# The last pair's finer t1 sums of x in a freed part of xT, and new unit orders for the second expert

## The chip, the core and the metric

The kernel runs on one core of a Trainium2 chip. The core has five engines that work at the same time: TensorE (PE, matrix products, with a row PEld for its weight loads), VectorE (DVE), ScalarE (ACT), GpSimd (POOL) and SyncE (SP, here a queue that issues DMAs). The on-chip memory SBUF has 128 partitions; products land in PSUM, eight banks of 128 x 512 fp32. The metric is device time in microseconds (us), lower is better.

## The reference

Two parts follow each other. The first is an attention with exponential features, whose output is the 4608 x 512 matrix x. The second is a layer of eight experts that all see every token; the weights P come from alternate normalisation of rows and columns.

```python
def phi(x):
    proj = np.einsum('bhsd,df->bhsf', x, w_phi)
    proj = proj - np.max(np.abs(proj), axis=-1, keepdims=True)
    return np.concatenate([np.exp(proj), np.exp(-proj)], axis=-1)
...
N, D = x.shape                  # 4608, 512; E = 8 experts, F = 1024
logits = x @ w_gate
logits = logits - logits.max()
P = np.exp(logits)
for _ in range(8):
    P /= P.sum(1, keepdims=True) + 1e-09
    P /= P.sum(0, keepdims=True) + 1e-09
    P *= N / E
out = np.zeros((N, D), dtype=np.float32)
for e in range(E):
    h = np.maximum(x @ w1[e], 0.0)
    ye = h @ w2[e]
    out += P[:, e:e + 1] * ye
```

## The kernel before

**Tiles.** x is kept transposed in bf16, xT, as four rows of 128 features by 4608 tokens. The tokens make nine groups of 512; groups 0 to 7 form four pairs, (0,1) to (6,7), and group 8 stands alone.

**Seven products for eight.** From the second expert on (e = 1, with `up7` and `down7`), both matrix products of an expert use Strassen's scheme in Winograd's form: of four blocks of each operand, some sums are made first, and seven products do the work of eight. `sums_x` makes the sums of x, once for all experts: t2, t3 and t4 go into tiles of the ring X, and t1 replaces a block of xT in place. From the third expert on (`up49`), three of these seven products ("11", "21" and t1 of x) are split once more in the same way, and for that `fine_x` makes four finer sums of each of the three blocks, into one more tile of the ring X. All of these are stored to DRAM (xd for t2 to t4, xi for the finer ones, xi6t being those of t1 of the pair (6,7)), and later experts load them back into xT, which is free then (`load_fine`). `sums_up` and `sums_down` make the sums of an expert's weights, `fine_up` the finer ones.

**Rings.** X has four tiles. In the second expert three of them hold t2, t3 and t4 of the pair at work until the products have read them. The fourth takes, one after another, the three sets of finer sums: each set has to be stored before the next can be written there. From the third expert on the ring's memory holds other things (K).

**Units.** An expert is a row of units: for each pair two (one for each half of the hidden features), and one for group 8. A unit's products of the first matrix are named x1, w1, x2, x3, w2, y1 and x4 with 0 or 1 behind, those of the second matrix, of a group that is one or two units back, X1, Y1, Z1, X2, X3, Z2, X4. A product goes into a PSUM bank, and ACT or DVE empties it: the products x4 add to a bank whose x3 result DVE has first to read with the addition at L1530. The results of the second matrix are added to acc, on DVE (L1860), or by ACT (L1872) and POOL (L1875).

**What sets the order.** `UNITS` holds, for each unit, a string in which steps are written; `turns` says which string each unit of each expert takes (entries 0 to 8 are the second expert's). From the strings a planner (`Plan`) makes the order of instructions on every engine: it goes through modelled time, and where several instructions could start, the one written first goes first. It knows the data that instructions read and write by keys: reads wait for the last write of a key, writes for its reads too. Each engine, and the SP and POOL queues, then work strictly in the planned order. The weights of the third expert (e = 2) are loaded by POOL (L517), behind its addition of step Y1 of group 4, and DVE makes their sums (T<-w, w<-w) in the last two units of the second expert.

**Places in xT.** `space` names a stretch of a row of xT that is used again once the products with that part of x are done. `FINE_W` are three such places for weight sums, `PLAIN_X` five and `FINE_X` four for loaded sums of x; `PLAIN_X.places[4]` is the first 1024 columns of the fourth row, which held features of the pair (0,1).

Of the kernel before, what the change touches and what calls it, by code (L numbers as in the profile page):

```python
# [12 lines left out]
ALU = mybir.AluOpType  # L13
# [113 lines left out]
class Links:  # L127
# [13 lines left out]
    def step(self, t, work):  # L141
        on = [n for n in range(2) if self.line[n] and self.line[n][0][0] <= t + 1e-9]
        later = [x[0][0] for n, x in enumerate(self.line) if x and n not in on]
        if not on:
            return (min(later), None, None) if later else None
        share = [1.0, 1.0]
        if len(on) == 2:
            a, b = (x[0][2] for x in self.line)
            all_ = (0.61 if a.turn else 0.84) / (a.unit + b.unit)
            share = [all_ * a.unit, all_ * b.unit]  # L150
        dt, n = min((work[n] / share[n], n) for n in on)
        if later and later[0] - t < dt:
            dt, n = max(later[0] - t, 0.0), None
        for i in on:
            work[i] -= dt * share[i]
        return t + dt, n, work
# [193 lines left out]
def kernel(  # L350
# [77 lines left out]
    def dma(queue, nbytes, rate, fn, r=(), w=()):  # L428

        speed, unit = LINK.get(rate, (rate, 40))  # L430
        if nbytes == 2 << 20:
            speed, unit = 400, 150
        o = plan.op(queue, 0.8 if queue == "POOL" else 0.6, 0.0, fn, r, w, (), nbytes / speed)
        o.turn, o.unit = rate == 148, unit
# [71 lines left out]
    def new(tag):  # L506
        return R[tag].new()
# [582 lines left out]
    def stage_g(b):  # L1090
# [11 lines left out]
    order = (  # L1102
        "lraeaepqbwlqaqawwabwmqlltnrbppnwqbppmrmanbqaqmwwacmpnpbccpwbtcnmqnaqbclupunm"
        "taumquglcapalbcpnqqdcenmucugbblnapmrcqdutabnqpmunpbambccddnqplanmqmducpblttb"
        "augnaqlnrbdcampcadmqeutunqcppmdcaqtdqabpbbmlrqtdnpmuaqualbnagnacctbmqulupran"
        "tdpmtdqcmdnpdabdancpcabbqmpumqbcdgnappqunburqcbugmmnqdcdanumupqbnucmcpnmbddp"
        "bqmpncncubncmmgccg"
    )
# [127 lines left out]
    def sub(eng, el, out_, x, y, op, r, w):  # L1236
        f = nc.vector if eng is dve else nc.gpsimd
        kw = {"shared": True} if eng is dve else {}
        eng(el * 0.5 if eng is dve else el * 1.04 + 128,
            lambda: f.tensor_tensor(out=out_(), in0=x(), in1=y(), op=op), r, w, **kw)  # L1240
# [30 lines left out]
    def fine_up(A, n):  # L1271

        f, r = A[n]
        t, key, first = FINE_W[n]

        def a(q, k):
            return lambda: f()[:, k, :].rearrange("p (f q c) -> p q f c", f=2, q=2)[:, q]

        def s(n):
            return lambda: t()[:, n]  # L1280

        def step(n, x, y, op, r, w):
            sub(dve, 256, s(n), x, y, op, r, [(key, n), *w])

        step(0, a(1, 0), a(1, 1), ALU.add, r, first)
        step(2, a(0, 0), a(1, 0), ALU.subtract, r, [])
        step(1, s(0), a(0, 0), ALU.subtract, [*r, (key, 0)], [])
        step(3, a(0, 1), s(1), ALU.subtract, [*r, (key, 1)], [])
        A[n + "*"] = t, [(key, i) for i in range(4)]
# [34 lines left out]
    def xall(gs):  # L1324
        return [k for g in gs for k in xkeys(g)]

    def space(row, at, n, names, dims, dtype=BF16):

        def make():
            t = xT[:, row, at:at + n]  # L1330
            t = t.bitcast(dtype) if dtype != BF16 else t
            return t.rearrange(f"p ({' '.join(names)}) -> p {' '.join(names)}",
                               **dict(zip(names, dims)))

        first = [k for p in range(at // 1024, (at + n - 1) // 1024 + 1) for k in xall(pairs[p])]
        return make, ("space", row, at), first

    class Turns:
# [4 lines left out]
        def next(self):  # L1343
# [9 lines left out]
    PLAIN_X = Turns([space(2 + i // 4, 1024 * (i % 4), 1024, "akc", (2, 2, 256))  # L1353
                     for i in range(5 if len(INNER) > 2 else 6)])
# [5 lines left out]
    Xi = {(g[0], n): dram.tile([128, 7, 256], BF16, name=f"xi{g[0]}{n}")  # L1360
          for g in pairs for n in INNER.values()}
# [3 lines left out]
    def fine_x(gs, n, b, r0):  # L1365

        g = gs[0]
        r = xall(gs) + ["late", *r0]
        dma("SP", 1 << 16, 160, lambda: nc.sync.dma_start(
            out=Xi[g, n][:, 0, :], in_=b()[:, 0, 0, :]), r, [("Xi", g, n, 0)])  # L1370
        dma("SP", 1 << 17, 160, lambda: nc.sync.dma_start(
            out=Xi[g, n][:, 1:3, :], in_=b()[:, :, 1, :]), r, [("Xi", g, n, 1)])
        y = new("X")

        def t(n):
            return lambda: y().rearrange("p a k c -> p (a k) c")[:, n]

        def blk(k, a):
            return lambda: b()[:, a, k, :]

        sub(dve, 256, t(0), blk(0, 1), blk(0, 0), ALU.subtract, r, [(y, 0), "order of X"])
        sub(dve, 256, t(2), blk(1, 1), blk(0, 1), ALU.subtract, r, [(y, 2)])
        sub(dve, 256, t(1), blk(1, 1), t(0), ALU.subtract, [*r, (y, 0)], [(y, 1)])
        sub(dve, 256, t(3), blk(1, 0), t(1), ALU.subtract, [*r, (y, 1)], [(y, 3)])
        dma("SP", 1 << 18, 160, lambda: nc.sync.dma_start(
            out=Xi[g, n][:, 3:7, :], in_=y().rearrange("p a k c -> p (a k) c")),
            [(y, i) for i in range(4)], [("Xi", g, n, 2)])

    def load_fine(gs):

        g, X = gs[0], {}

        def move(name, d, r, turns, part=None):
            t, key, first = turns.next()
            X[name] = t, [key]
            size = (512 if part else 1024) if turns is PLAIN_X else 1792
            dma("SP", size << 8, 160, lambda: nc.sync.dma_start(
                out=t()[:, 0:part] if part else t(), in_=d()), r, [key, *first, "order of X"])

        if len(gs) == 1:  # L1400
            for n in (2, 3, 4):
                move(f"t{n}", lambda n=n: Xd[g, n][:, 0:1], [("Xd", g, n)], PLAIN_X, 1)
            return X
        for n in ("11", "t1", 2, "21", 3, 4, "22"):
            if n == "22" or n in ("11", "21", "t1") and n not in INNER.values():
                move(n, lambda n=n: Xp[g, n], [("Xp", g, n, a) for a in range(2)], PLAIN_X)
            elif isinstance(n, int):
                move(f"t{n}", lambda n=n: Xd[g, n], [("Xd", g, n)], PLAIN_X)
            else:
                move(n, lambda n=n: Xi[g, n], [("Xi", g, n, i) for i in range(3)], FINE_X)  # L1410
        return X
# [379 lines left out]
    def down7(e, g, H, B7):  # L1791
# [173 lines left out]
    def next_down():  # L1965
        if early:
            return early.pop(0)
        e, g, H, B7, w2, ns = wait.pop(0)
        d = down8(e, g, H, w2) if (e, g) == (E - 1, 7) else down7(e, g, H, B7)
        d["slots"] = ns  # L1970
        return d
# [7 lines left out]
    for e in range(1, E):  # L1979
# [13 lines left out]
        for n, gs in enumerate(turn):  # L1993
            if (e, n) == (1, 4):
                plan.inorder = 1
            X = nextX if e == 1 else load_fine(gs)
# [27 lines left out]
    last = next_down()  # L2024
# [34 lines left out]
```

## Time and profile before

| | |
|---|---|
| median of 3 runs | 1010.66 us (1009.91 to 1011.52) |
| profiled execution, its span | 1008.8 us |
| PE busy | 994.0 us (99%) |
| DVE busy | 898.6 us (89%) |
| ACT busy | 812.8 us (81%) |
| POOL busy | 447.6 us (44%) |

The profile is of one execution; it gives the span from the first to the last instruction, which is 1.86 us less than the median of the runs, and no other time of its own. Rows name the engine, the line of the kernel, the operation, and the tiles written and read, as in `X<-xT`. "Idle before" with an engine or DMA behind it says what the engine waited for. The record of a matmul or of a DVE instruction ends after the next one has begun, so groups of equal instructions are read by their starts.

### The profile page before, as it was taken

To read this page: it belongs to the slowest core of one execution; us is meant where nothing else is said; L and a number is where in the kernel's file an instruction comes from. 1 tells how busy PE (TensorE), PEld (TensorE's weight loads), DVE (VectorE), ACT (ScalarE), POOL (GpSimd) and SP (SyncE) were. 2 spreads that over 40 slices of the span, in tenths; PEclk is the share of its full clock that TensorE was granted. 3 is DMA by queue.
4 is the path that set the end of the run, shared out by engine and by line. 5 is a ranking of instruction groups with operands and counts; after the bars stand their busy time and mean duration, and the time that the engine had idled before them with its cause. 6 is when DMAs were issued, how large, how long until landed. Compare 5 with 4: busy or idle time off the path is not lost.

```text
span 1008.8 us, 23309 instructions
## 1 busy us (share of the span) xinstructions
PE 994.0 (99%) x8376; PEld 727.7 (72%) x8376; DVE 898.6 (89%) x1999; ACT 812.8 (81%) x1930; POOL 447.6 (44%) x514
## 2 busy tenths in 40 slices
PE   7899999999999999999999999999999999999998
PEld 5666666644566877777777877787778777787775
DVE  7999998987888998899989898989889988989886
ACT  7999999845979788878878788777887888778874
POOL 5778674400133344434444444444443444344443
PEclk9999999999999999999999999999999999999999
DMA  9999999181136423282327133632246222724653
GB/s 249 183 202 183 157 153 144 38 170 56 53 121 143 147 97 98 84 184 96 109 98 170 44 100 131 130 127 98 97 117 177 97 98 84 147 79 142 208 174 126
DMA packets 129748, 128.86 MB, mean 128 GB/s; under 512 B 55776, under 2 KB 98272, under 8 KB 129632
## 3 DMA queue, kind: packets, MB, share of 16 engines
q1 hardware_dynamic: 97680, 103.33, 36.3%
q0 software_dynamic: 31648, 23.86, 16.9%
q8 instruction: 65, 1.06, 0.5%
q14 instruction: 51, 0.42, 0.2%
q10 hardware_dynamic: 304, 0.20, 0.1%
HBM read 122.50 MB, written 19.53 MB: 141 GB/s over the span
## 4 chain that ended last, share of the span: by engine, by line
PE 92%; DVE 3%; ACT 2%; DMA 2%; issue 1%; POOL 0%; DVEq 0%
PE ps L1466 41%; PE ps L1475 20%; PE ps L622 17%; PE ps L1607 11%; PE ps L905 2%; DMA xi6t<-X 1%; DMA xi<-X 1%; PE ps L752 1%; ACT q L618 0%; DVE m L614 0%; ACT k L618 0%; DVE wx L614 0%; DVE X L1240 0%; DMA acc<-in_k_dram 0%; DVE hs L1676 0%
## 5 line engine op out<-in xcount | busy, mean ns | idle before, releaser
L1875 POOL TENSOR_TENSOR acc<-acc,hx 128x512 f32<-128x512 f32 x186 | 236.1, 1276 | 404.7 <-ACT hx L1872 135.0
L1466 PEld LDWEIGHTS <-hs 128*128 128x128 bf16 x1984 | 194.1, 98 | 46.4 <-issue 0.2
L1872 ACT ACTIVATE hx<-ps,P 128x256 f32<-128x256 f32 x372 | 158.9, 483 | 53.4 <-PE ps L1466 52.0
L1860 DVE SCALAR_TENSOR_TENSOR acc<-ps,P,acc 128x256 f32<-128x256 f32 x372 | 162.2, 478 | 30.2 <-PE ps L1466 28.2
L1475 PE MATMUL ps<-xT,T 128*128 128x512 bf16 x608 | 171.0, 379 | 0.0
L1466 PEld LDWEIGHTS <-hx 128*128 128x128 bf16 x1488 | 145.6, 98 | 24.9
L1466 PE MATMUL ps<-hx,hs 128*128 128x256 bf16 x992 | 144.3, 273 | 0.0
L1676 DVE CUSTOM_DVE_ANT_0 hs<-ps,U 128x512 bf16<-128x512 f32 x192 | 124.7, 684 | 11.3 <-PE ps L1475 6.6
L1607 PE MATMUL ps<-xT 128*128 128x256 bf16 x576 | 125.4, 272 | 0.0
L1475 PEld LDWEIGHTS <-T 128*128 128x128 bf16 x672 | 65.8, 98 | 40.6
L1682 ACT ACTIVATE hs<-ps 128x512 bf16<-128x512 f32 x96 | 55.9, 598 | 41.7 <-PE ps L1475 40.2
L1466 PE MATMUL ps<-wx,hs 128*128 128x256 bf16 x560 | 78.4, 273 | 0.0
L622 PE MATMUL ps<-w,hx 128*128 128x512 bf16 x288 | 73.0, 379 | 0.0
L622 PE MATMUL ps<-xT,w 128*128 128x512 bf16 x288 | 72.9, 379 | 0.0
L1466 PE MATMUL ps<-wx,hx 128*128 128x256 bf16 x496 | 72.3, 273 | 0.0
L1676 DVE CUSTOM_DVE_ANT_0 hs<-ps,X 128x512 bf16<-128x512 f32 x96 | 65.1, 684 | 7.8 <-PE ps L1607 6.9
L1466 PE MATMUL ps<-hx 128*128 128x256 bf16 x496 | 71.2, 273 | 0.0
L1607 PEld LDWEIGHTS <-xT 128*128 128x128 bf16 x576 | 56.3, 98 | 17.5
L1466 PE MATMUL ps<-w,hx 128*128 128x256 bf16 x432 | 62.2, 273 | 0.0
L614 DVE TENSOR_REDUCE m<-ps 128x4 f32<-128x512 f32 x88 | 58.8, 680 | 3.7 <-PE ps L622 1.9
L1672 ACT COPY X<-ps 128x512 f32<-128x512 f32 x96 | 58.6, 610 | 2.5 <-DVE ps L1650 2.5
L1466 PE MATMUL ps<-w,hs 128*128 128x256 bf16 x432 | 60.2, 273 | 0.0
(174 smaller groups left out, 2256.0 us busy)
## 6 DMA issues: line engine op xcount, KB each, us to landing
xT<-xi SPq DMA_DIRECT2D x48, 448.0 KB, 4.6
xT<-xd SPq DMA_DIRECT2D x72, 256.0 KB, 4.0
wx<-in_moe_w_dram POOLq DMA_DIRECT2D x8, 1024.0 KB, 11.2
v_m<-in_v_dram SPq DMA_DIRECT2D x15, 512.0 KB, 5.2
out_dram<-acc SPq DMA_DIRECT2D x14, 512.0 KB, 3.0
w<-in_moe_w_dram POOLq DMA_DIRECT2D x6, 1024.0 KB, 11.0
xT<-xp SPq DMA_DIRECT2D x24, 256.0 KB, 2.8
qk<-in_k_dram POOLq DMA_DIRECT2D x12, 256.0 KB, 5.4
```

The costliest lines, as they stand in the source:

```text
L614: dve(el, lambda: nc.vector.tensor_reduce(out=dst(), in_=src(), axis=AX.X, op=ALU.max, apply_absolute_value=True), r, w)
L622: nc.tensor.matmul(out_, lhsT=lhsT, rhs=rhs, start=start, stop=stop)
L905: pe(65, lambda j=j: nc.tensor.matmul(pn()[:, j * D1:j * D1 + D1], lhsT=s["T"][x]()[:, j % 2, 2 * h + j // 2, :] if j < 4 else r["T"][x]() ...
L1466: pe(256, lambda i=i, k=k, z=z: nc.tensor.matmul(bank()[:, 256 * i:256 * i + 256], lhsT=lhs(k, i), rhs=rhs(k), start=first and z, stop=k = ...
L1475: pe(512, lambda k=k: nc.tensor.matmul(bank().rearrange("p (a b) -> p a b", a=2), lhsT=lhs(k), rhs=rhs(k), start=first and k == 0, stop=k ...
L1607: pe(256, lambda: nc.tensor.matmul(halves_of(bank[q], n)(), lhsT=lhs(), rhs=t()[:, rhs, :], start=start, stop=True, skip_group_check=True) ...
L1672: act(512, lambda: nc.scalar.copy(out=flat(to[q])(), in_=bank[q]()), [bank[q]], [(to[q], 0), (to[q], 1)])
L1676: dve(515, lambda: nc.vector._custom_dve(ADD_SAT, out=out_(q, i, j), in0=bank[q]().rearrange("p (a b) -> p a b", a=2), in1=to[q](), s0=3.0 ...
L1682: act(512, lambda: nc.scalar.activation(out=out_(q, i, j), in_=bank[q]().rearrange("p (a b) -> p a b", a=2), func=ACT.Relu, bias=0.0, scal ...
L1860: dve(320, lambda n=n, ts=ts: nc.vector.scalar_tensor_tensor(out=acc[g][:, ts, 256 * j:256 * j + 256], in0=bank()[:, 256 * n:256 * n + 256 ...
L1872: act(370, lambda n=n: nc.scalar.activation(out=u()[:, n, :], in_=bank()[:, 256 * n:256 * n + 256], func=ACT.Copy, bias=0.0, scale=P[:, 4 ...
L1875: pool(695, lambda: nc.gpsimd.tensor_tensor(out=acc[g][:, 2 * i:2 * i + 2, 256 * j:256 * j + 256], in0=acc[g][:, 2 * i:2 * i + 2, 256 * j: ...
```

## The change

Two things change in the code, and one in the tables. In `fine_x`, the four finer sums of t1 of the pair (6,7) are written to `PLAIN_X.places[4]` instead of a tile of X, and stored from there. In `fine_up`, sum 2 gets the same first wait as sum 0, for the readers of the part of xT that it overwrites. Of `UNITS`, the entries 4 to 8 are written anew (those that follow are only wrapped differently).

```diff
@@ fine_up
         step(0, a(1, 0), a(1, 1), ALU.add, r, first)
-        step(2, a(0, 0), a(1, 0), ALU.subtract, r, [])
+        step(2, a(0, 0), a(1, 0), ALU.subtract, r, first)
         step(1, s(0), a(0, 0), ALU.subtract, [*r, (key, 0)], [])
@@ fine_x
-        y = new("X")
-
-        def t(n):
-            return lambda: y().rearrange("p a k c -> p (a k) c")[:, n]
+        last = g == 6 and n == "t1"
+        if last:
+            y, key, first = PLAIN_X.places[4]
+            keys = [[key, *first]] * 4
+        else:
+            y, first = new("X"), []
+            keys = [[(y, i)] for i in range(4)]
+
+        def t(i):
+            return lambda: y().rearrange("p a k c -> p (a k) c")[:, i]
...
-        sub(dve, 256, t(0), blk(0, 1), blk(0, 0), ALU.subtract, r, [(y, 0), "order of X"])
+        sub(dve, 256, t(0), blk(0, 1), blk(0, 0), ALU.subtract, r, [*keys[0], "order of X"])
...
-            [(y, i) for i in range(4)], [("Xi", g, n, 2)])
+            [k[0] for k in keys], [("Xi", g, n, 2)])
@@ UNITS
-        "x10 x11 w10 x21 x20 Z1 w11 X1 X2 x30 X3 y11 Y1 x31 w21 x41 x40 X4 Z2 w20 y10",
...
+        "x11 w11 w10 x10 X1 y11 x20 Z1 x30 X2 x21 x40 x31 X3 Z2 w20 Y1 w21 X4 x41 y10",
```

The planner makes of this another order of all engines from about 287 us of the trace before to about 354; ahead and behind, the order is as it was. Lines of the change behind `fine_x` are 6 higher (L1530 is L1536, L1860 is L1866). Three places on DVE follow. In the rows, `[waits ...]` names the semaphores an instruction waits on (DMAHW0 to 7 are those of the SP queue, taken in turn; DMASW6 is one of POOL's loads), L1240 is any sum, `w_5163` and `w_5170` are the same tile, w1 of the third expert.

DVE about the end of the last unit of the pair (4,5), where the finer sums of the next pair, (6,7), are made; before, those of t1 are the four into X with the wait on DMAHW0, which is the store of the "21" sums:

```order
L1240 TENSOR_TENSOR hx<-hs,hx 128x512
L1860 SCALAR_TENSOR_TENSOR acc_82<-ps,P,acc_82 128x256 [waits PE_49,Activation_49]
L1860 SCALAR_TENSOR_TENSOR acc_82<-ps,P,acc_82 128x256
L1240 TENSOR_TENSOR X<-xT 128x256 [waits DMAHW0_49,DVE_49]
L1240 TENSOR_TENSOR X<-xT 128x256
L1240 TENSOR_TENSOR X<-xT,X 128x256 [waits DVE_49] x2
L1240 TENSOR_TENSOR hx<-hs 128x512 [waits PE_49] x2
```

The same place now; the four into xT are those of t1:

```order
L1240 TENSOR_TENSOR X<-xT 128x256 [waits DMAHW7_49]
L1240 TENSOR_TENSOR X<-xT 128x256
L1240 TENSOR_TENSOR X<-xT,X 128x256 [waits DVE_49]
L1240 TENSOR_TENSOR xT<-xT 128x256
L1240 TENSOR_TENSOR X<-xT,X 128x256 [waits DVE_49]
L1240 TENSOR_TENSOR xT<-xT 128x256
L1240 TENSOR_TENSOR hx<-hs,hx 128x512
L1240 TENSOR_TENSOR xT<-xT 128x256 [waits DVE_49]
L1866 SCALAR_TENSOR_TENSOR acc_81<-ps,P,acc_81 128x256 [waits PE_49]
```

The t1 sums moved up among the "21" sums (X<-xT and X<-xT,X here), and no DMA is waited for on their account.

DVE at the first sum of group 8, t3 (X<-xT 128x512), before:

```order
L1860 SCALAR_TENSOR_TENSOR acc_82<-ps,P,acc_82 128x256
L1530 ISA hs<-ps,U 128x2x256
L1530 ISA hs<-ps,U 128x2x256 [waits PE_49]
L1240 TENSOR_TENSOR X<-xT 128x512 [waits DMAHW1_49]
L1240 TENSOR_TENSOR hx<-hs,hx 128x512 [waits DVE_49]
L1240 TENSOR_TENSOR xT<-xT 128x2x256 [waits DVE_49]
```

and now:

```order
L1240 TENSOR_TENSOR hx<-hs 128x512
L1240 TENSOR_TENSOR hx<-hs 128x512 [waits PE_49]
L1240 TENSOR_TENSOR X<-xT 128x512 [waits DMAHW0_49]
L1240 TENSOR_TENSOR hs<-hs 128x2x256 [waits DVE_49]
L1536 ISA hs<-ps,U 128x2x256 [waits PE_49,Activation_49]
L1536 ISA hs<-ps,U 128x2x256 [waits PE_49]
```

The sum moved ahead of all four additions of the first unit of the pair (6,7), and waits on DMAHW0 (the store of the "21" sums) where it waited on DMAHW1 (the store of the t1 sums).

DVE at the first sums of the weights of the third expert, in the last unit of the pairs, before:

```order
L1240 TENSOR_TENSOR hs<-hs 128x2x256
L1240 TENSOR_TENSOR hx<-hx,hs 128x512
L1240 TENSOR_TENSOR T<-w_5163 128x1024 [waits DMASW6_49]
L1240 TENSOR_TENSOR X<-xT 128x512 [waits DVE_49,PE_49]
L1240 TENSOR_TENSOR hx<-hs,hx 128x512 [waits DVE_49]
L1240 TENSOR_TENSOR w_5163<-w_5163 128x2x512 [waits DVE_49]
L1240 TENSOR_TENSOR xT<-w_5163 128x256
L1530 ISA hs<-ps,U 128x2x256 [waits PE_49,Activation_49]
L1240 TENSOR_TENSOR X<-xT,X 128x512 [waits DMAHW4_49,DVE_49,PE_49]
```

and now:

```order
L1240 TENSOR_TENSOR hx<-hs,hx 128x512 [waits DVE_49]
L1240 TENSOR_TENSOR X<-xT 128x512 [waits PE_49]
L1240 TENSOR_TENSOR T<-w_5170 128x1024 [waits DMASW6_49]
L1240 TENSOR_TENSOR xT<-w_5170 128x256
L1240 TENSOR_TENSOR w_5170<-w_5170 128x2x512 [waits DVE_49]
L1240 TENSOR_TENSOR xT<-w_5170 128x256
L1240 TENSOR_TENSOR xT<-xT,w_5170 128x256 [waits DVE_49]
L1536 ISA hs<-ps,U 128x2x256 [waits PE_49,Activation_49]
L1240 TENSOR_TENSOR X<-xT,X 128x512 [waits DMAHW4_49,PE_49]
L1536 ISA hs<-ps,U 128x2x256
```

Group 8's second sum (X<-xT 128x512) and one sum of H moved ahead of T<-w, and two more finer weight sums ahead of the additions. On PE, the last product of step Y1 of group 4, behind which POOL issues the weight loads, stands three 256-column matmuls later than before.

More of the change, by code (lines that the diff above doesn't have):

```diff
@@ L1372, in fine_x @@
             out=Xi[g, n][:, 1:3, :], in_=b()[:, :, 1, :]), r, [("Xi", g, n, 1)])
-        y = new("X")
-        def t(n):
-            return lambda: y().rearrange("p a k c -> p (a k) c")[:, n]
+        last = g == 6 and n == "t1"
[7 more added lines that the diff above has]
+            return lambda: y().rearrange("p a k c -> p (a k) c")[:, i]
         def blk(k, a):
             return lambda: b()[:, a, k, :]
-        sub(dve, 256, t(0), blk(0, 1), blk(0, 0), ALU.subtract, r, [(y, 0), "order of X"])
-        sub(dve, 256, t(2), blk(1, 1), blk(0, 1), ALU.subtract, r, [(y, 2)])
-        sub(dve, 256, t(1), blk(1, 1), t(0), ALU.subtract, [*r, (y, 0)], [(y, 1)])
-        sub(dve, 256, t(3), blk(1, 0), t(1), ALU.subtract, [*r, (y, 1)], [(y, 3)])
+        sub(dve, 256, t(0), blk(0, 1), blk(0, 0), ALU.subtract, r, [*keys[0], "order of X"])
+        sub(dve, 256, t(2), blk(1, 1), blk(0, 1), ALU.subtract, r, keys[2])
+        sub(dve, 256, t(1), blk(1, 1), t(0), ALU.subtract, [*r, keys[0][0]], keys[1])
+        sub(dve, 256, t(3), blk(1, 0), t(1), ALU.subtract, [*r, keys[1][0]], keys[3])
         dma("SP", 1 << 18, 160, lambda: nc.sync.dma_start(
             out=Xi[g, n][:, 3:7, :], in_=y().rearrange("p a k c -> p (a k) c")),
-            [(y, i) for i in range(4)], [("Xi", g, n, 2)])
+            [k[0] for k in keys], [("Xi", g, n, 2)])
     def load_fine(gs):
```

20 rows, old and new, of the table UNITS are left out of this document.

## The prediction

> **What bounds the kernel now.** I read the page's busy times, then the busy times by stretch, the waits, the chain and the order of time. The page first:
>
> ```profile
> span 1008.8 us, 23309 instructions
> PE 994.0 (99%) x8376; PEld 727.7 (72%) x8376; DVE 898.6 (89%) x1999; ACT 812.8 (81%) x1930; POOL 447.6 (44%) x514
> ```
>
> TensorE (PE) is busy for 99% of the span, and it has the full clock (the 1.00 behind the engines in the next table). Only its idle time can be won, so the next table asks where that lies. Columns are the stretch, its length, the busy time of PE, its weight loads, DVE, ACT and POOL, the granted clock, the DMA share and GB/s.
>
> ```profile
> 0.00:60.00 60.00, 50.27 (x530) 34.65 (x531) 54.11 (x117) 54.31 (x135) 41.86 (x72) 1.00 1.19 221
> ...
> 220.00:320.00 100.00, 99.64 (x600) 58.03 (x599) 83.60 (x209) 75.12 (x147) 18.43 (x16) 1.00 0.28 89
> 320.00:340.00 20.00, 19.37 (x142) 13.62 (x140) 18.33 (x48) 16.27 (x33) 6.16 (x5) 1.00 1.04 268
> 340.00:990.00 650.00, 649.72 (x5200) 508.49 (x5198) 585.91 (x1259) 520.28 (x1267) 283.21 (x271) 1.00 0.41 116
> ```
>
> The change reorders work from about 287 to 354 us alone; before and behind, the instructions stand as they did. There PE is idle for 0.63 us, all of it between 320 and 340. The 9.73 us at the start and the 3.83 us behind 990 are not touched. The idle 0.63 us has one owner, found in the waits from 290 to 336 us (in total, times, longest):
>
> ```profile
> DVE X L1240 <- DMA xi6t<-X: 1.0, 1, 1.0
> PE ps L1475 <- DVE hs L1530: 0.6, 1, 0.6
> ```
>
> The chain ties the two waits together:
>
> ```profile
> 317.00 7.75 DMA xi6t<-X
> ...
> 324.77 0.42 DVE X L1240
> ...
> 329.13 0.42 DVE X L1240
> 329.55 0.61 DVE hs L1530
> ...
> 330.20 0.59 PE ps L1475 x2
> ```
>
> The store of the last pair's t1 sums (xi6t<-X) takes 7.75 us to land. It holds the fourth tile of the ring of sum tiles, because the other three hold the pair's t2, t3 and t4, which products still read. So group 8's first sum waits for it on VectorE (DVE), everything behind it on DVE is late, and at last PE waits for a DVE addition that empties its bank. What PE loses is more than the 0.6 us of that row, since a matmul's record overlaps the next one:
>
> ```profile
> 321.84 1.03 PE L1475 MATMUL ps<-X,wx 128*128 128x512 bf16 x4
> 322.71 1.89 PE L1475 MATMUL ps<-xT,wx 128*128 128x512 bf16 x8
> 329.20 0.38 PE L1475 MATMUL ps<-xT,T 128*128 128x512 bf16 x1
> 330.20 1.19 PE L1475 MATMUL ps<-X,wx 128*128 128x512 bf16 x4 [0.62 <-DVE hs L1530]
> 331.67 1.04 PE L1466 MATMUL ps<-hx,hs 128*128 128x256 bf16 x8
> ```
>
> From the first row, matmuls of 512 columns follow each other every (1.03 - 0.38) / 3 = 0.217 us; from the last, those of 256 every (1.04 - 0.27) / 7 = 0.11 us. The one behind 329.20 was due at 329.42 and began at 330.20: 0.78 us. The next four took 1.19 instead of 1.03: 0.16 us. The stall costs 0.94 us.
>
> **The change, part by part.** First DVE in order of time (start, length of the group, idle time before it). A record overlaps the next by some 0.08 us: two additions take 1.28 in the last row, so one holds the engine for 0.60, and a sum of 0.42 holds it for 0.34.
>
> ```profile
> 313.08 1.01 DVE L1240 TENSOR_TENSOR hx<-hs,hx 128x512 bf16<-128x512 bf16 x1
> 315.17 0.88 DVE L1860 SCALAR_TENSOR_TENSOR acc<-ps,P,acc 128x256 f32<-128x256 f32 x2 [1.08 <-PE ps L1466]
> 315.96 0.49 DVE L1240 TENSOR_TENSOR X<-xT 128x256 bf16<-128x256 bf16 x2
> 316.36 0.61 DVE L1240 TENSOR_TENSOR X<-xT,X 128x256 bf16<-128x256 bf16 x2
> ...
> 318.14 0.42 DVE L1240 TENSOR_TENSOR hx<-hs 128x512 bf16<-128x512 bf16 x1 [0.83 <-PE ps L1466]
> ...
> 324.77 0.42 DVE L1240 TENSOR_TENSOR X<-xT 128x512 bf16<-128x512 bf16 x1 [1.01 <-DMA xi6t<-X]
> 325.12 0.42 DVE L1240 TENSOR_TENSOR hx<-hs,hx 128x512 bf16<-128x512 bf16 x1
> ...
> 326.46 0.69 DVE L1240 TENSOR_TENSOR T<-w 128x1024 bf16<-128x1024 bf16 x1
> ...
> 329.47 1.28 DVE L1530 CUSTOM_DVE_ANT_0 hs<-ps,U 128x512 bf16<-128x512 f32 x2
> ```
>
> The SP queue and POOL in order of time:
>
> ```profile
> 308.03 4.68 SPq L1385 DMA_DIRECT2D xi<-X  x2
> 317.00 0.32 SPq L1385 DMA_DIRECT2D xi6t<-X  x1
> 325.23 4.67 SPq L1422 DMA_DIRECT2D xd<-X  x3
> ```
>
> ```profile
> 314.79 1.27 POOL L1875 TENSOR_TENSOR acc<-acc,hx 128x512 f32<-128x512 f32 x1 [0.98 <-ACT hx L1872]
> 316.00 1.69 POOL L517 DMA_DIRECT2D w<-in_moe_w_dram  x2
> ```
>
> Transfers by size and time to landing, from 305 to 314 us in the first row, from 315 to 332 in the others; the last line is the first weight load alone:
>
> ```profile
> xi<-X SPq DMA_DIRECT2D x2, 256.0 KB, 2.0
> ...
> xd<-X SPq DMA_DIRECT2D x3, 128.0 KB, 4.0
> xi6t<-X SPq DMA_DIRECT2D x1, 256.0 KB, 7.8
> ...
> DMA to landing us min/median/max: 9.5/9.5/9.5
> ```
>
> *The four t1 sums.* They read and write the same shapes on the same engine, some 0.2 us each in the rows at 315.96 and 316.36; only the target is xT, where the weights' finer sums already go. Cost 0. They need no tile of the ring now, so they move up to stand among the "21" sums, about 2 to 3 us earlier. A sum that falls beside POOL's addition can stretch as the row at 313.08 does (1.01 against 0.42), by 0.6 us; the 1.08 us that DVE then waits for PE (315.17) cover it. Without that cover the price would be those 0.6 us on DVE.
>
> *The t1 store.* Same bytes, same queue, issued some 2 us earlier, ahead of the weight loads of 316.00; it should land in about 2.0 us, as its two sisters, where it took 7.8 beside the loads. Nothing waits for it until that part of xT is loaded again by the third expert. The swap of the t4 store with a first part of xi6t on SP moves two small stores by one place; both are issued near 305, long before anybody needs them: 0.
>
> *Group 8's first sum.* It now waits for the "21" store, the second xi<-X, issued at 308.03 + 4.68 - 0.32 = 312.4 and landed 2.0 us later, so it runs in DVE's wait at 318.14. DVE's 1.01 us of idle time go. Its store (128 KB) moves from 325.2 to about 318, into the weight loads; it may take up to 7.8 us instead of 4.0, and lands by 326, before the last of group 8's sums is made at 329.13. Nothing waits: 0.
>
> *What is late next: the weights.* DVE reaches the first weight sum (T<-w) at 326.46 - 1.01 (idle) - 0.35 (the first sum moved ahead) + 0.33 + 0.34 (group 8's second sum and one sum of H, which now stand ahead of it) = 325.77. The first load lands at 316.00 + 9.5 = 325.5. POOL issues it behind the addition of step Y1, whose last product stands three 256-column matmuls later in the new order, so at 325.5 + 0.33 = 325.83 if nothing else changes. From T<-w to the end of the second addition that PE needs, DVE has 0.60 + 0.60 for two weight sums, 3 x 0.20 for finer ones, 0.60 + 0.34 + 0.60 + 0.69: 4.03 us, so it ends at 329.86. PE comes to that product 26 wide and 16 narrow matmuls behind 322.71: 26 x 0.217 + 16 x 0.11 = 7.4, at 330.1. Margin 0.25 us. Bounds on PE: 0 with the load as it was, 0.94 if the load is late enough to bring the whole stall back. The row of this very load is the nearest, so I take 0.1.
>
> The landing of 7.8 against 2.0 us shows that the store and the load, issued by SP and POOL, slow each other. The Trainium skill, "DMA: Bandwidth & Descriptors" (Issuing engines are not separate DMA queues), says that transfers started by different engines run on the same 16 DMA engines and interleave. By that rule the load, freed of 256 KB and given 128 KB, would land earlier than 325.5, and this term would be 0, so 0.1 us less; the sum here doesn't use it.
>
> *The wait added to finer weight sum 2.* It repeats the wait of sum 0 of the same weights, on the same engine, which comes first on DVE in the new order. So it is never the later of the two: 0, and at worst some of the 0.25 us of margin.
>
> *The unit orders.* The same products in another order from 287 to 354 us. No row shows them. Below: no gain beyond the 0.94 us, since PE has no other idle time there. Above: one more stall like this one, 0.94. The row 340 to 990 has 0.28 us idle in 650 under orders of this kind, the nearest guide, so 0.
>
> Sum: -0.94 + 0.1 = -0.84 us, a span of 1008.0. The runs' median, 1010.66, stands 1.86 above the span; I keep that: 1009.8 us. A measurement of this kernel tells about 0.2% (2.0 us) from no change, so this would be within 0.2%.
>
> **The rivals.**
>
> *The weights take the store's place.* If the first load lands between 326.1 and 327, T<-w waits instead of X<-xT, and PE stalls by 0 to 0.94 us again: 1010.0 to 1010.7. For it: the wait and the arrival stand within 0.1 us of each other. Against: the store leaves the load's way.
>
> *Slower: the load is late by microseconds.* The loads of all experts:
>
> ```profile
> DMA to landing us min/median/max: 8.4/11.2/17.2
> ```
>
> If this first load took 17.2 us from 316.33, it would land at 333.5. DVE would stop for 7.7 us with every bank addition behind it, PE for 7.5: 1010.66 - 0.94 + 7.5 = 1017.2. It makes the kernel measurably slower from a landing of 12.6 us on (325.77 + 0.25 + 0.94 + 2.02 = 328.98). For it: the median of 11.2. Against: that holds the second load of each pair too, which queues behind the first, and this load took 9.5 with more beside it.
>
> *The stall stays.* If PE waits at 330.2 for another reason than DVE's lateness, the time is 1010.7. Against: DVE has no idle time between 324.77 and 330.2, and 1.01 us of lateness give 0.94 on PE.
>
> **Numbers.** The likeliest case, the stall gone or nearly, 0.72; the weights take its place, 0.12; the stall stays, 0.05; slower by the load or by a new order that costs over 2.9 us of stalls, 0.08; over 2.02 us faster, 0.03: more than the 0.94 us of stall, thus only by chance of runs. Faster 0.03, within 0.2% 0.89, slower 0.08. The range goes from the full gain at the lowest of three runs, 1009.72 - 0.75 = 1009.0, rounded down to 1008.9, to no gain at the highest of the runs, 1011.5.
>
> **What would show it.** In the new profile: the wait of DVE X on xi6t gone, xi6t<-xT landing in 2 to 3 us, group 8's first sum near 318, and PE dense from 320 to 340. The reason falls if PE waits there for a DVE addition though DVE never stood idle; the forecast falls if T<-w waits for w by over 3 us, or if PE shows idle time between 287 and 320 or from 340 to 354 that it didn't have.

## The result, and the profile after

The changed kernel takes 1008.76 us in the median of 20 runs (1007.66 to 1009.50). The kernel before, run beside it, takes 1010.14 (1009.40 to 1011.52, 20 runs). The ratio is 0.9982, with a 95% interval of 0.9976 to 0.9988, so the change saves 1.2 to 2.4 us. The forecast was 1009.8, with a range from 1008.9 up. The direction was right, the gain was too small, and the median lies just below the range.

The profiled execution took 1008.87 us. The top of its page, and two rows of the table by stretches, with the columns as in the prediction:

```profile
span 1007.1 us, 23304 instructions
PE 993.4 (99%) x8376; PEld 728.2 (72%) x8376; DVE 897.1 (89%) x1999; ACT 813.2 (81%) x1930; POOL 447.0 (44%) x514
...
320.00:340.00 20.00, 20.00 (x151) 14.56 (x150) 19.28 (x50) 17.00 (x36) 3.46 (x4) 1.00 1.00 254
340.00:990.00 650.00, 650.00 (x5201) 508.60 (x5200) 585.16 (x1259) 521.14 (x1268) 285.00 (x272) 1.00 0.40 116
```

Between 320 and 340 TensorE has lost its 0.63 us of idle time. The row below it matters as much: from 340 to 990 TensorE is busy for 650.00 of 650 us, where it was 649.72. There both kernels give it the same work from 354 us on.

The first of the two answers the prediction. VectorE, SP, the transfers and TensorE around the old stall (start and length of a group; for the transfer, size and time to landing; in the fourth fence, one load's time to landing):

```profile
313.41 0.88 DVE L1240 TENSOR_TENSOR xT<-xT 128x256 bf16<-128x256 bf16 x1
314.22 0.41 DVE L1240 TENSOR_TENSOR hx<-hs,hx 128x512 bf16<-128x512 bf16 x1
315.30 0.88 DVE L1866 SCALAR_TENSOR_TENSOR acc<-ps,P,acc 128x256 f32<-128x256 f32 x2 [0.68 <-PE ps L1472]
...
316.76 0.42 DVE L1240 TENSOR_TENSOR X<-xT 128x512 bf16<-128x512 bf16 x1
...
325.67 0.69 DVE L1240 TENSOR_TENSOR T<-w 128x1024 bf16<-128x1024 bf16 x1
```

```profile
314.32 0.32 SPq L1391 DMA_DIRECT2D xi6t<-xT  x1
```

```profile
xi6t<-xT SPq DMA_DIRECT2D x1, 256.0 KB, 3.0
```

```profile
DMA to landing us min/median/max: 9.3/9.3/9.3
```

```profile
329.02 0.59 PE L1481 MATMUL ps<-X,wx 128*128 128x512 bf16 x2
329.45 0.59 PE L1481 MATMUL ps<-xT,wx 128*128 128x512 bf16 x2
329.88 0.59 PE L1481 MATMUL ps<-X,wx 128*128 128x512 bf16 x2
```

The t1 store leaves at 314.3, ahead of the weight loads, and lands in 3.0 us. Group 8's first sum waits for nothing at 316.76. The first weights are there 9.3 us after the issue at 316.14, thus at 325.4, just before the sum T<-w at 325.67. TensorE's groups of two follow each other every 0.43 us, with no gap.

The other part stands where the change moved nothing. TensorE around 704 us, before and then after:

```profile
704.40 0.59 PE L1475 MATMUL ps<-xT,wx 128*128 128x512 bf16 x2
704.83 0.38 PE L1466 MATMUL ps<-wx,hx 128*128 128x256 bf16 x2
705.36 0.59 PE L1475 MATMUL ps<-xT,wx 128*128 128x512 bf16 x2
```

```profile
703.28 0.59 PE L1481 MATMUL ps<-xT,wx 128*128 128x512 bf16 x2
703.71 0.38 PE L1472 MATMUL ps<-wx,hx 128*128 128x256 bf16 x2
703.93 0.59 PE L1481 MATMUL ps<-xT,wx 128*128 128x512 bf16 x2
```

Two narrow matmuls take 2 x 0.11 us. So the next was due at 705.05 before and came at 705.36: a gap of 0.31 us, which is gone after. The same happens at 967 us, with 0.29 us. I call gap what the start of a matmul lies behind the start of the last one, beyond 0.217 us (512 columns) or 0.11 (256). The gaps that the two kernels don't share are, in us: 0.07 at 303, 0.78 and 0.16 at 329 to 331, 0.31 at 705, 0.29 at 967. They sum to 1.61. The prediction had 0.94 of them.

### The profile page after: what moved, and what is told of

It reads as the page before. It is cut to its first block, busy times and chain, and to the rows that moved or that the text cites. A ratio compares the mean times of both kernels' runs of the same rounds, so it can differ in the third digit from the quotient of the medians.

```text
span 1007.1 us, 23304 instructions
## 1 busy us (share of the span) xinstructions
PE 993.4 (99%) x8376; PEld 728.2 (72%) x8376; DVE 897.1 (89%) x1999; ACT 813.2 (81%) x1930; POOL 447.0 (44%) x514
## 3 DMA queue, kind: packets, MB, share of 16 engines
q8 instruction: 65, 1.06, 0.4%
## 4 chain that ended last, share of the span: by engine, by line
PE 92%; ACT 3%; DVE 2%; DMA 2%; issue 1%; POOL 0%; SPq 0%; DVEq 0%
PE ps L1472 42%; PE ps L1481 21%; PE ps L622 15%; PE ps L1613 11%; PE ps L905 2%; DMA xp<-xT 1%; ACT k L618 1%; ACT q L618 1%; DMA xi<-X 1%; PE ps L752 0%; DVE m L614 0%; ACT wx L618 0%; DVE wx L614 0%; DMA acc<-in_k_dram 0%; PE ps L934 0%
## 5 line engine op out<-in xcount | busy, mean ns | idle before, releaser
L1866 DVE SCALAR_TENSOR_TENSOR acc<-ps,P,acc 128x256 f32<-128x256 f32 x372 | 162.0, 477 | 29.8 <-PE ps L1472 28.1
```

The source lines that it names most:

```text
L1866: dve(320, lambda n=n, ts=ts: nc.vector.scalar_tensor_tensor(out=acc[g][:, ts, 256 * j:256 * j + 256], in0=bank()[:, 256 * n:256 * n + 256 ...
```

## The experiments

### Are the gaps at 705 and 967 us part of the kernel, or of one execution?

Both kernels again, unchanged.

> The kernel before once more, unchanged. Theory A (the change removes one stall of 0.94 us, and what the times fell beyond that, some 0.5 to 0.8 us, is idle time of TensorE that one execution has and another has not, as at 705 and 967 us of the profile before): the stall near 329 us stands in the new profile too, 0.8 to 1.1 us long, and the gaps at 705 and 967 us (0.3 us each) are missing or stand elsewhere. Theory B (the stall itself varies and is larger in most executions than in the one profiled): the stall comes out at 1.2 us or more. Theory C (the gaps at 705 and 967 us belong to the order of the instructions of before): they stand at the same places, 0.3 us each. Ratio to before 1.000 within 0.0005 by all three.

> The changed kernel once more. A: TensorE dense from 320 to 340 us again; some gaps of 0.1 to 0.3 us waiting for nothing that the profile shows may stand anywhere; ratio 0.9980 to 0.9990. B: ratio 0.9982, no gaps but those common to both profiles. C: no gaps at 705 and 967 us in this profile either, ratio 0.9982.

The kernel before: 1010.31 us, ratio 1.0003 [0.9994, 1.0012]. The changed kernel: 1008.45 us, ratio 0.9986 [0.9977, 0.9995]. TensorE in the new profile of the kernel before:

```profile
328.49 0.38 PE L1475 MATMUL ps<-xT,T 128*128 128x512 bf16 x1
329.49 1.19 PE L1475 MATMUL ps<-X,wx 128*128 128x512 bf16 x4 [0.62 <-DVE hs L1530]
...
704.12 0.38 PE L1466 MATMUL ps<-wx,hx 128*128 128x256 bf16 x2
704.65 0.59 PE L1475 MATMUL ps<-xT,wx 128*128 128x512 bf16 x2
```

All four gaps come back to within 0.01 us: 0.78 and 0.17 at the stall, 0.31 near 704, 0.29 near 966. The second profile of the changed kernel has none of them. Theories A (idle time of one execution) and B (a stall that varies) fall; the gaps belong to the program (C). Why an unchanged order should have them in one kernel and not in the other was still open.

### The place alone

The kernel before with each engine's order kept: the planner still believes in the ring's tile, only the addresses change.

```diff
         y = new("X")
+        z = PLAIN_X.places[4][0] if g == 6 and n == "t1" else y
...
-            return lambda: y().rearrange("p a k c -> p (a k) c")[:, n]
+            return lambda: z().rearrange("p a k c -> p (a k) c")[:, n]
...
-            out=Xi[g, n][:, 3:7, :], in_=y().rearrange("p a k c -> p (a k) c")),
+            out=Xi[g, n][:, 3:7, :], in_=z().rearrange("p a k c -> p (a k) c")),
```

> The kernel before, each engine's order kept as it is, with only the place of the last pair's t1 sums changed (row 3 of xT in place of the ring's fourth tile). A: DVE's wait on the xi6t store and the stall of 0.94 us go although the store still takes 7 to 8 us to land beside the weights; 0.9 us faster than before, ratio 0.9991; if the new unit orders save the rest, the changed kernel stays 0.5 to 0.8 us ahead of this one. B: ratio 0.9982, level with the changed kernel. C: 0.9991, with the gaps at 705 and 967 us still there.

1008.75 us, ratio 0.9991 [0.9982, 0.9999]. Its store, VectorE and TensorE:

```profile
xi6t<-xT SPq DMA_DIRECT2D x1, 256.0 KB, 7.8
```

```profile
322.36 0.41 DVE L1240 TENSOR_TENSOR X<-xT 128x512 bf16<-128x512 bf16 x1
...
324.40 0.69 DVE L1240 TENSOR_TENSOR T<-w 128x1024 bf16<-128x1024 bf16 x1 [0.28 <-DMA w<-in_moe_w_dram]
...
327.42 1.28 DVE L1530 CUSTOM_DVE_ANT_0 hs<-ps,U 128x512 bf16<-128x512 f32 x2
```

```profile
327.88 0.38 PE L1475 MATMUL ps<-xT,T 128*128 128x512 bf16 x1
328.15 1.19 PE L1475 MATMUL ps<-X,wx 128*128 128x512 bf16 x4
```

The store is as slow as ever, but nobody waits for it. The wait for the weights that the rival spoke of does appear, 0.28 us on VectorE. TensorE loses 0.05 at 328.15 (due at 328.10), where it needs the first of the two additions at 327.42, done at 327.42 + 0.68 = 328.10. It loses another 0.17 behind it (1.19 for four matmuls again): it needs the second addition two matmuls later, 2 x 0.217 = 0.43 us, and VectorE makes the two 0.60 us apart. So the 0.17 follows whenever TensorE has to wait for the first addition, whatever made that late. Here the weights' wait costs 0.22 in all, where the store's cost 0.94. The gaps at 705 and 967 us are gone, in an order of instructions that is that of before, and a new one of 0.14 us stands at 446. That contradicts C as I had put it: the gaps follow neither the time nor the order.

What does differ is a count. Without the wait for the ring's tile, VectorE needs one wait instruction less: its records in the trace, wait instructions included, are 2588 in the kernel before, 2587 here and 2585 in the changed kernel.

### Which instruction is late?

VectorE around 703 us, before and then after:

```profile
702.20 0.73 DVE L1240 TENSOR_TENSOR hs<-hs 128x1024 bf16<-128x1024 bf16 x1
703.42 0.69 DVE L1676 CUSTOM_DVE_ANT_0 hs<-ps,U 128x512 bf16<-128x512 f32 x1 [0.49 <-ACT ps L1733]
704.03 0.68 DVE L1676 CUSTOM_DVE_ANT_0 hs<-ps,X 128x512 bf16<-128x512 f32 x1
704.63 0.68 DVE L1676 CUSTOM_DVE_ANT_0 hs<-ps,U 128x512 bf16<-128x512 f32 x1
```

```profile
701.08 0.74 DVE L1240 TENSOR_TENSOR hs<-hs 128x1024 bf16<-128x1024 bf16 x1
701.95 0.69 DVE L1682 CUSTOM_DVE_ANT_0 hs<-ps,U 128x512 bf16<-128x512 f32 x1
```

The addition begins 1.22 us behind the sum ahead of it, where after the change it is 0.87: 0.35 us late. The additions behind it are late with it, and TensorE's matmul at 705.36 waits for the last of them (704.63 + 0.68 = 705.31). The releaser that the row names, ScalarE's copy at L1733, is not the cause: in the changed kernel that copy runs from 701.66 to 702.27, and the addition begins at 701.95, in its midst. In the records of the wait instructions, which the timeline leaves out, the wait ahead of this addition is over at 702.99, and the addition begins 0.43 us later; in the kernel with the place alone it begins 0.08 us after its wait.

The late addition is VectorE's record number 1855, counted from 0. The other, at 964.25, is number 2495, and 2495 - 1855 = 640 = 5 x 128. The page of before has a row that fits (queue, packets, MB, share):

```profile
q8 instruction: 65, 1.06, 0.5%
q14 instruction: 51, 0.42, 0.2%
```

Of the 23309 records of before, 16771 are TensorE's (8376 matmuls, 8395 weight loads and waits), and 65 loads of 16 KB fit them: one for each 258. The other 6538 share 51 loads of 8 KB: one for each 128. Theory D: VectorE's program comes in pieces of 128 instructions, and the first of a piece is 0.35 us late. Mostly VectorE is still busy, or ahead of the others, and nobody sees it. In the kernel before, two of these places fall on additions that TensorE is waiting for.

### One instruction more, three instructions more

Writes of one column to a tile that is no longer read (at 372.5 us in the traces); all else is the same.

```diff
+                if (e, n, fp) == (2, 0, 1):
+                    last = [d for d in plan.ops if d.eng == "DVE"][-1]
+                    last.fn = lambda f=last.fn: (f(), [nc.vector.memset(
+                        colw[:, i:i + 1], 0.0) for i in range(1)])[0]
                 if dn is not None:
                     dn["out"]()
```

The changed kernel gets `range(3)`.

> The kernel before with one more instruction on VectorE (a write of one column to a tile that nobody reads any more) at about 365 us; nothing else differs. Theory D (TensorE's gaps of 0.31 and 0.29 us at 705 and 967 us are VectorE waiting for its own instructions: each 128th instruction of its program comes 0.35 us late, and before has two of these in front of an addition that TensorE waits for; the change lost three VectorE wait instructions and so moved these places): the stall at 329 us stays with 0.79 and 0.16 us, the gaps at 705 and 967 us go, a small one may appear elsewhere; 0.4 to 0.6 us faster than before, ratio 0.9994 to 0.9996. Theory E (the gaps come from how the stall at 329 us shifts the engines against the DMAs): they stay, ratio 1.000.

> The changed kernel with three more such instructions on VectorE at about 365 us, so that its program from there on has the length that it has in the kernel before. D: no stall at 329 us, but gaps of 0.31 and 0.29 us in the work that the kernel before does at 705 and 967 us (here near 704 and 965 us); 0.6 us slower than the changed kernel, ratio to before 0.9990. E: no such gaps, ratio 0.9984.

Before with one more: 1009.56 us, ratio 0.9994 [0.9986, 1.0003]. After with three more: 1008.98 us, ratio 0.9992 [0.9983, 1.0001]. TensorE in the first, then TensorE and VectorE in the second:

```profile
328.50 0.38 PE L1475 MATMUL ps<-xT,T 128*128 128x512 bf16 x1
329.46 1.19 PE L1475 MATMUL ps<-X,wx 128*128 128x512 bf16 x4 [0.58 <-DVE hs L1530]
...
704.09 0.38 PE L1466 MATMUL ps<-wx,hx 128*128 128x256 bf16 x2
704.31 0.59 PE L1475 MATMUL ps<-xT,wx 128*128 128x512 bf16 x2
```

```profile
704.13 0.38 PE L1472 MATMUL ps<-wx,hx 128*128 128x256 bf16 x2
704.65 0.59 PE L1481 MATMUL ps<-xT,wx 128*128 128x512 bf16 x2
```

```profile
702.72 0.69 DVE L1682 CUSTOM_DVE_ANT_0 hs<-ps,U 128x512 bf16<-128x512 f32 x1 [0.48 <-ACT ps L1739]
```

One instruction takes both gaps from the kernel before and leaves its stall; three instructions give them to the changed kernel, with 0.31 and 0.29 us, and no stall. D holds, and E (a shift against the DMAs) falls: in the changed kernel nothing else had moved. The times alone wouldn't settle it, since both intervals hold 1.000 and the second overlaps that of the changed kernel (0.9977 to 0.9995); the profiles do.

### The orders alone, and the place with the old orders

The first is the kernel before with the five new rows of UNITS; the second is the changed kernel with the five old ones.

```diff
-        "x10 x11 w10 x21 x20 Z1 w11 X1 X2 x30 X3 y11 Y1 x31 w21 x41 x40 X4 Z2 w20 y10",
+        "x11 w11 w10 x10 X1 y11 x20 Z1 x30 X2 x21 x40 x31 X3 Z2 w20 Y1 w21 X4 x41 y10",
...
```

> The kernel before with only the five new unit orders, the t1 sums still in the ring's fourth tile. Between the last t1 sum and group 8's first sum DVE now has some 3.5 us of work (four additions and two accumulations) where before had nearly 7 us, and the store takes 7.8 us to land if it runs beside the weights: A and B: DVE waits some 4 us there, TensorE stalls nearly as long, ratio 1.003 (1013 us). If the store is issued ahead of the weights and lands in 3 us: no wait, ratio 0.999. C: the new orders save 0.7 us on their own, ratio 0.9993 or less if the wait is hidden.

> The changed kernel with the five old unit orders. Its order of instructions is not that of before, since the planner moves group 8's first sum ahead, and its VectorE program has as many instructions as that of before. D: no stall of 0.9 us at 329 us if the old orders feed TensorE as well as the new; gaps of 0.31 and 0.29 us near 704 and 965 us; ratio 0.9990 (1009.1 us). E: no gaps at 704 and 965 us, ratio 0.9984. If the new orders are needed: stalls between 287 and 354 us, over 1010 us.

The orders alone: 1018.23 us, ratio 1.0084 [1.0070, 1.0098]. The place with the old orders: 1010.38 us, ratio 1.0002 [0.9993, 1.0011]. The waits of the first from 312 to 345 us, and a row of its VectorE:

```profile
DVE hs L1530 <- ACT U L1523: 3.0, 1, 3.0
PEld L1475 <- issue: 2.9, 3, 2.0
DVE X L1240 <- DMA xi6t<-X: 2.7, 1, 2.7
```

```profile
328.91 0.68 DVE L1240 TENSOR_TENSOR T<-w 128x1024 bf16<-128x1024 bf16 x1
```

With the sums still in the ring, VectorE waits 2.7 us for the store (I had said some 4), and the work behind it is late for long: T<-w comes 3.2 us later than in the changed kernel, and TensorE's gaps from 324 to 392 us sum to 10.3 us. I had counted the one stall, not what piles up behind it: I expected 1013 us, 3 above before, and it is 8 above.

The place with the old orders has no stall at 329 us, and the gaps of 0.31 and 0.29 us at 705 and 967, as D says of a program with 2588 records of VectorE. But it has seven gaps between 353 and 381 us that sum to 1.9 us: once the first sum no longer waits, the planner puts the work in another order, and the old unit orders don't fit that. So the new orders save 1.9 us of gaps in the kernel as it is planned. Against the place alone, which keeps the old plan, they save 0.28: the 0.22 of the weights' wait and the 0.07 at 303. That is within noise: the place alone, three lines and no new order, has a median of 1008.75 us, level with the changed kernel's 1008.76 and 1008.45, and the ratios of the same round, 0.9991 and 0.9986, have intervals that overlap.

### The weight loads held back

The kernel before with its orders kept, and the third expert's two loads waiting for the store.

```diff
+        store, loads = self.hold
+        done = [o for o in done if o not in loads]
+        i = done.index(store) + 1
+        done[i:i] = loads
...
+                if o in loads:
+                    tc.add_manual_dep(
+                        o.ins.ins, store.ins.ins.name, mybir.DependencyInfo(
+                            mybir.DependencyClass.Sync, mybir.DependencyReason.DATA),
+                        reason="the store first")
```

> The kernel before, orders kept, with the third expert's two weight loads made to wait until the xi6t store has landed. If the loads are what makes the store land late: the store lands in about 3 us, VectorE no longer waits for it, and the first weights land near 329.5 us in place of 325.5 (loads issued at about 320.1, 9.4 us to land), so that VectorE waits some 4.5 us for them and TensorE stalls 4 to 5 us in place of 0.95: 1013.5 to 1015 us, ratio 1.0035 to 1.005; more if late work piles up on VectorE behind the wait. If the store is slow by itself: it lands in 7 to 8 us, and the loads come 8 us late, 1018 us or more.

1012.52 us, ratio 1.0026 [1.0017, 1.0035]. The store, VectorE and TensorE:

```profile
xi6t<-X SPq DMA_DIRECT2D x1, 256.0 KB, 2.0
```

```profile
327.75 0.69 DVE L1249 TENSOR_TENSOR T<-w 128x1024 bf16<-128x1024 bf16 x1 [2.53 <-DMA w<-in_moe_w_dram]
```

```profile
328.94 0.38 PE L1485 MATMUL ps<-xT,T 128*128 128x512 bf16 x1
331.50 1.19 PE L1485 MATMUL ps<-X,wx 128*128 128x512 bf16 x4 [2.19 <-DVE hs L1540]
```

Without the loads beside it the same store lands in 2.0 us in place of 7.75, so it was the loads that made it slow. VectorE waits 2.53 us for the weights, less than the 4.5 I expected, because the store landed earlier than I had assumed, and the first load was quicker too (8.5 us; I had taken 9.4). TensorE's gap is 331.50 - 329.16 = 2.34 us, with 0.17 behind it. So what VectorE waits for at this place arrives at TensorE nearly whole, the two gaps taken together: 0.28 gave 0.22, 1.01 gave 0.94, 2.53 gave 2.51.

### The account

Gaps of TensorE from 300 us on that the kernels don't all share, in us, from the profiled executions, and the medians. (Ahead of 300 us the gaps differ between executions of one kernel, by 0.3 us at 227.)

| kernel | records of VectorE | 303 | 329 | 330 | 446 | 705 | 967 | other | time, us |
|---|---|---|---|---|---|---|---|---|---|
| before | 2588 | 0.07 | 0.78 | 0.16 | | 0.31 | 0.29 | | 1010.14 |
| changed | 2585 | | | | | | | | 1008.76 |
| place alone | 2587 | 0.07 | 0.05 | 0.17 | 0.14 | | | | 1008.75 |
| before, 1 more | 2589 | 0.07 | 0.74 | 0.17 | | | | | 1009.56 |
| changed, 3 more | 2588 | | | | | 0.31 | 0.29 | | 1008.98 |
| place, old orders | 2588 | 0.07 | | | | 0.31 | 0.29 | 1.9 | 1010.38 |
| loads held | 2588 | 0.07 | 2.34 | 0.17 | | 0.31 | 0.31 | | 1012.52 |

The two gaps stand in every kernel of this table with 2588 records and in no other. From before to the changed kernel the gaps give -1.61 us; the medians -1.38 (20 runs) and -1.67 (the repeat, against 1010.12). "Place, old orders" lacks three gaps that all the others have, at 534 to 587 us with 0.32 together; its gaps put it 0.63 above before, its median 0.26. "Loads held" is 0.8 us above what its gaps say; its runs scatter from 1011.55 to 1014.59, and one profile can't tell how late the weights are in the others.

## Why the prediction was right and wrong

- **The stall: right, mechanism and size.** VectorE's wait for the store is what stalled TensorE, and its 0.94 us are gone in the changed kernel. In the place alone 0.22 of them come back, but by the wait for the weights.
- **The t1 sums: right.** One of them is stretched beside POOL's addition to 0.88 us, by 0.6 as said, and the 0.68 us in which VectorE then waits for TensorE (315.30) cover it.
- **The t1 store: right in effect.** It took 3.0 us, not 2.0, and nobody waits for it. Group 8's first sum came at 316.8 (said: near 318).
- **The weights: 0, not 0.1.** T<-w at 325.67 (said: 325.77), the load there at 325.4. The rule of the Trainium skill, "DMA: Bandwidth & Descriptors" (Issuing engines are not separate DMA queues), that transfers of different issuers share the DMA engines had given this 0. The trace agrees, if only by 0.2 us (9.3 us to land, 9.5 before). The held loads agree more plainly: the store is 5.75 us quicker alone, and the first load lands in 8.5.
- **The unit orders, put at 0: mis-sized a little.** They gave the 0.07 us at 303, and with them the wait for the weights, which costs 0.22 in the place alone, doesn't appear. My bound, "no gain beyond the 0.94 us, since PE has no other idle time there", was false, and busy times couldn't show it: TensorE counts as busy for all of the time from 300 to 310 us, since the 0.27 us record of a narrow matmul covers the 0.18 us to the next start. (The 0.36 us of idle time in the quoted row from 220 to 320 is another gap, at 228.)
- **The step that failed** is the first: idle time "between 320 and 340" alone, because "before and behind, the instructions stand as they did". The row from 340 to 990 showed 0.28 us of idle time in my own table. I took it for the ordinary idle time of such orders; it was two gaps, of which a matmul's long record hides half. And though the order behind 354 us is the same, VectorE's program is three wait instructions shorter, which moved its late places off the additions that TensorE waits for. This term, -0.60 us, was missing: the gaps removed are 0.94 + 0.07 + 0.60 = 1.61 us. The two gaps stood in the profile of before; that the change would remove them could only be told by someone who knew what made them.
- **The base** was high by as much. The sum was put on the median of three runs, 1010.66; twenty runs give 1010.14. Of the 1.06 us by which 1009.82 (before rounding) missed, 0.52 are this, and 0.54 the gain, 1.38 in place of 0.84. The profiled execution came to the stall at 330.20 us, its repeat at 329.49: the slowness of the first lies ahead of the stall, where executions of one kernel differ.
- **The rivals.** The weights did take the store's place where the order was kept: 0.28 us on VectorE, 0.22 on TensorE, within the 0 to 0.94 that was said. That the stall stays for another reason fell: it went with the wait. The slower case has the price that was worked out for it, nearly one for one; it needs loads that are late by microseconds, and they weren't.

## What to carry to other kernels

Read a stall from the starts of neighbouring instructions, not from busy shares: where records overlap, half of a gap of 0.3 us is hidden, and all of one of 0.07. Where an edit adds or takes away instructions, waits among them, it also moves where the later pieces of that engine's program begin, and on a kernel this dense that can be worth much of the edit, 0.60 of 1.61 us here; a spare instruction tells whether it does. And when a change brings its own fitted order, run it with the old orders as well, and once with the old plan kept: here the old orders, planned anew, took back the whole gain (1010.38 us), while the place alone in the old plan has nearly all of it (1008.75).

## What the runs showed of the hardware

VectorE's first instruction of a piece of 128 began 0.40 to 0.43 us after its wait had ended, where the same instruction in another kernel needs 0.04 to 0.08: at the records 1855 and 2495 of the kernel before, and, in the kernel with the place alone, at 1215 = 1855 - 5 x 128, the accumulation at 445.10 us that makes the new gap at 446. Where VectorE is still busy, little or nothing of it shows. At 2239 = 1855 + 3 x 128 of the place alone the instruction ahead covers all but 0.03 us, and record 1343 of before starts 0.45 us behind the one ahead, as it does in the changed kernel, where it begins no piece.

The Trainium skill, "Runtime: NRT & Kernel Launch" (Instruction fetch mechanics), says that programs are loaded in blocks of 16 KiB, 256 instructions, and that crossing into the next one is mostly hidden. For TensorE the page agrees (65 loads of 16 KB, one for each 258 instructions). For the other engines the trace shows 8 KB and 128, and where TensorE waits on VectorE the crossing is not hidden: 0.60 us in two places.

What fills the 0.35 us isn't shown. It isn't a load under way: in the trace of before the 8 KB loads nearest to the two late instructions begin 0.64 and 0.91 us behind their starts (704.06 and 965.17 us), and none is running when they are due. So a new piece and a new load come together, but the late instruction doesn't wait for that load.

The profile gave these delays other names. TensorE's loss at 705 us stands as "issue", time in which nothing is waited for, though it waits for an addition on VectorE; and VectorE's row names a copy on ScalarE that the addition doesn't need.
